# Six batches of attention results multiplied by the reciprocals of their sums in the second part of the kernel, behind the load, and the ones matmuls taking GpSimd's sum last

## The chip, the cores and the metric

The kernel runs on one core of a Trainium2 chip. The metric is the device time of that core in microseconds (us), the median of the runs shown. Times within one execution come from a hardware profile of a single run. TensorE is called PE (its weight loads PEld), VectorE DVE, ScalarE ACT, GpSimd POOL, and SyncE, which only issues DMAs here, SP.

## The reference, cut to what matters

```python
# q, k, v: (8 batches, 8 heads, 1152, 64)
q_pool = q.reshape(B, H, 576, 2, 64).mean(axis=3)
scores = scale * q_pool @ k.T
attn   = exp(scores - max(scores)) / (sum(exp(...)) + 1e-9)
x      = attn @ v                         # as (8, 576, 512)
theta  = x @ w_theta
y      = w_tok_r @ (x * cos(theta)) + w_tok_i @ (x * sin(theta))
u      = x + y
out    = u + max(u @ w_ch, 0)
```

The division by the sum can be made anywhere between the matmul with v and the first use of x. Where it is made is what this case is about.

## The kernel before

**Part one** is the attention, for 32 pairs of heads, four pairs to a batch, one after the other in steps of about 25 us. The matmuls of a pair are the row maxima (`pm`, `px`, `py`; reduced by DVE into `mx`), the scores (`pe`), the weighted values (`pa`), and a few matmuls with ones (`pns`) that sum the exponentials over partitions. ACT writes the exponentials (`pc`), POOL adds seven of the nine `pc` tiles of each half into `ss` (L443), and the ones matmuls take `ss` and the last two `pc` tiles (L479).

From the sums, a chain of small steps makes the factors: `norm_spread` and `norm_load` turn the row of sums through DRAM, DVE takes the reciprocal (`rc`, L506), `norm_save` stores it (`ro`), `norm_bcast` (L519) reads it back with two DMAs into all 128 partitions (`dn`, 128x576), `norm_out` (L528) multiplies the pair's result `xu` by it on DVE, and `norm_store` (L542) stores `xu` in DRAM as `xd[b]`.

**Part two** is the rest, batch by batch, in cycles of about 55 us. `xload` (L183, L186) loads a batch as `xT` (128 x 4 slices x 640 columns for an even batch, which also holds the last 64 columns of the next one; 576 for an odd one) into one of two tiles. `xhi` (ACT, L196) and `xlo` (POOL, L200) split each slice in two for the theta matmuls (`pth`, L844); `xblock` (DVE, L825) transposes it in blocks of 32 for a store to `xbd[b]` (L826), from where `xnload` (L834) fetches it in the other layout. A chain on DVE and ACT (L866 to L901) makes the products `Z`, POOL their low halves (L905); the token matmuls (`py`, L932) add them up, `uadd` (L948) adds `xT`, the channel matmuls (`pr`, L971) and `relu` (L984) follow, and `oblock` (L992, L995) transposes and stores the output. So `uadd` of batch b - 2 is the last to read the `xT` tile that batch b gets.

All five engines work in the order in which the program is written. That order is made by numbers: each step is entered with a position (`at` in part one, 18 positions a pair; `at2` in part two, 56 positions a batch) and the steps are written in order of their positions. SP too is one queue: a DMA that waits for its data holds back every DMA written behind it. PE's banks of PSUM are handed on in turn, so a late reader (`relu`, `uadd`, a DVE maximum) makes a later matmul wait.

## Time and profile before

| | |
|---|---|
| median of 3 runs | 1280.24 us (1278.96 to 1281.43) |
| the profiled execution, whole | 1281.45 us |
| its span in the profile | 1279.7 us |
| PE busy over the span | 1237.6 us, 97% |
| DVE, ACT, POOL busy | 942.3, 671.6, 746.2 us |
| part one (until the last `pns`) | 0 to 834 us |
| part two | 834 to 1280 us |

The profiled execution is 1.21 us above the median, and 1.75 us of it lie outside the span. The profile's chain of work that ended last is 82% PE; busy shares of the other engines are averages over two parts that load them differently. POOL is at work most of part one and little in part two, DVE 86% of part one and some 60% of part two.

### The profile page before, as it was taken

The page shows a single profiled execution, that of the slowest core. Times are in us where ns is not written, and L with a number is a line of the kernel's source. Part 1 is how long each engine was busy: PE and PEld are TensorE (multiplying, and loading weights), DVE is VectorE, ACT ScalarE, POOL GpSimd, SP SyncE. Part 2 cuts the span into 40 slices and gives each one's busy share as a digit, 9 for nine tenths or more (in the row PEclk, how much of TensorE's full clock was granted, in tenths as well). Part 3 has the DMA queues.
Part 4 walks back from the last instruction along what each step waited for, and adds up shares of the span by engine and source line. Part 5 has one row for each costly group of instructions (what it writes and reads, how often), then busy time and mean ns, then how long its engine had stood idle before and what let it go on. Part 6 is the DMA issues. An engine that isn't in the chain of part 4 may idle for free.

```text
span 1279.7 us, 29400 instructions
## 1 busy us (share of the span) xinstructions
PE 1237.6 (97%) x11619; PEld 1002.2 (78%) x11619; DVE 942.3 (74%) x1370; ACT 671.6 (52%) x1161; POOL 746.2 (58%) x536
## 2 busy tenths in 40 slices
PE   3999999999999999999999999999999999999998
PEld 2777777767777777777777677788999999999998
DVE  6878888888888888888888887455565656647453
ACT  1566566656656665665666565555443443444331
POOL 0598768787786878787787767624323233232320
PEclk7999999999999999999999999999999999999999
DMA  5746554556555465555556541324635435354332
GB/s 92 129 84 129 105 115 109 120 118 143 107 105 116 102 130 113 110 104 123 107 116 113 106 89 52 99 74 108 134 49 127 90 76 128 49 132 83 81 54 38
DMA packets 488763, 129.88 MB, mean 101 GB/s; under 512 B 458672, under 2 KB 459632, under 8 KB 488624
## 3 DMA queue, kind: packets, MB, share of 16 engines
q1 hardware_dynamic: 488624, 127.99, 48.3%
q8 instruction: 91, 1.49, 0.5%
q14 instruction: 48, 0.39, 0.1%
HBM read 97.21 MB, written 29.52 MB: 99 GB/s over the span
## 4 chain that ended last, share of the span: by engine, by line
PE 82%; DVE 10%; DMA 3%; issue 3%; ACT 1%; SPq 1%; POOL 0%; DVEq 0%; ACTq 0%; POOLq 0%
PE pa L457 19%; PE pe L430 19%; PE py L932 17%; PE pr L971 8%; PE pth L844 8%; PE pm L375 6%; DVE mx L382 4%; PE pns L479 4%; DVE qk L292 2%; DMA qk<-in_k_dram 2%; PE px L392 1%; DVE wf L601 1%; DVE mx L397 1%; DMA nmr<-nt 1%; DMA qn<-in_q_dram 1%
## 5 line engine op out<-in xcount | busy, mean ns | idle before, releaser
L443 POOL TENSOR_TENSOR ss<-ss,pc 128x576 f32<-128x576 f32 x314 | 463.6, 1477 | 52.5 <-ACT pc L433 32.2
L382 DVE TENSOR_REDUCE mx<-pm 128x2 f32<-128x768 f32 x384 | 356.7, 952 | 96.0 <-PE pm L375 94.5
L433 ACT ACTIVATE pc<-pe 128x576 f32<-128x576 f32 x576 | 349.7, 652 | 74.7 <-PE pe L430 61.3
L457 PE MATMUL pa<-pc,vn 128*64 128x288 f32 x2304 | 300.4, 410 | 0.4 <-ACT pc L433 0.4
L457 PEld LDWEIGHTS pa<-pc,vn 128*64 128x64 f32 x2304 | 156.8, 137 | 108.8 <-issue 5.7
L932 PE MATMUL py<-wtk,Z 128*128 128x288 f32 x1728 | 233.8, 296 | 0.0
L932 PEld LDWEIGHTS py<-wtk,Z 128*128 128x128 f32 x1728 | 232.3, 189 | 1.3
L905 POOL TENSOR_TENSOR Z<-ab,Z 128x512 fp32r<-128x512 f32 x40 | 52.1, 1302 | 259.4 <-ACT Z L901 221.9
L430 PE MATMUL pe<-hi 64*128 64x288 f32 x1152 | 182.0, 311 | 0.3 <-DVE lo L360 0.2
L430 PE MATMUL pe<-nmr,oner 64*128 64x288 f32 x1152 | 171.2, 292 | 0.0
L430 PE MATMUL pe<-lo,hi 64*128 64x288 f32 x1152 | 170.6, 291 | 0.0
L430 PE MATMUL pe<-hi,lo 64*128 64x288 f32 x1152 | 170.6, 291 | 0.0
L443 POOL TENSOR_TENSOR ss<-pc,pc 128x576 f32<-128x576 f32 x64 | 91.7, 1433 | 126.0 <-ACT pc L433 125.6
L375 PE MATMUL pm<-hi 64*128 64x384 f32 x768 | 145.8, 377 | 16.1 <-ACT hi L349 5.8
L430 PEld LDWEIGHTS pe<-hi 64*128 64x128 f32 x1152 | 109.2, 185 | 24.1 <-issue 7.5
L375 PEld LDWEIGHTS pm<-hi 64*128 64x128 f32 x768 | 73.2, 187 | 64.0 <-DVE mx L382 16.5
L349 ACT CAST hi<-pt 128x768 fp32r<-128x768 f32 x64 | 56.2, 879 | 114.0 <-DVE pt L321 105.4
L430 PEld LDWEIGHTS pe<-lo,hi 64*128 64x128 f32 x1152 | 109.9, 186 | 0.0
L430 PEld LDWEIGHTS pe<-hi,lo 64*128 64x128 f32 x1152 | 109.4, 185 | 0.0
L430 PEld LDWEIGHTS pe<-nmr,oner 64*128 64x128 f32 x1152 | 109.1, 185 | 0.0
L971 PEld LDWEIGHTS pr<-us,wch 128*128 128x128 f32 x768 | 104.2, 188 | 1.6
L971 PE MATMUL pr<-us,wch 128*128 128x288 f32 x768 | 105.2, 296 | 0.0
(100 smaller groups left out, 1417.6 us busy)
## 6 DMA issues: line engine op xcount, KB each, us to landing
vn<-in_v_dram SPq DMA_DIRECT2D x32, 576.0 KB
qn<-in_q_dram SPq DMA_DIRECT2D x124, 144.0 KB
qk<-in_k_dram SPq DMA_DIRECT2D x124, 144.0 KB
dn<-ro SPq DMA_DIRECT2D x64, 144.0 KB
xd<-xu SPq DMA_DIRECT2D x32, 288.0 KB
xT<-xd SPq DMA_DIRECT2D x8, 1152.0 KB
xn<-xbd SPq DMA_DIRECT2D x140, 64.0 KB
out_dram<-ub SPq DMA_DIRECT2D x124, 72.0 KB
```

What stands on the lines that cost most here:

```text
L349: nc.scalar.copy(hi, src)
L375: nc.tensor.matmul(pm[:, h, 0:W], hi[hs, Q0 + j * P : Q0 + (j + 1) * P], hi[hs, K0[3 * g] : K0[3 * g] + W], start=True, stop=True,)
L382: nc.vector.tensor_reduce(mx[:, j : j + 5 : 4, g : g + 1], pm[:, :, 0:W], AX.X, ALU.max)
L430: nc.tensor.matmul(pe[:, h, 0:HALF], w[hs], x[hs], start=(n == 0), stop=(n == 3))
L433: nc.scalar.activation(pcs[u, kt], pe[:, :, 0:HALF], AF.Exp, scale=SC)
L443: eng.tensor_tensor(st["ss", u], first, st["pc"][u, kt], ALU.add)
L457: nc.tensor.matmul(pa[hs, 0, 0:HALF], st["vn"][:, h, (kt + 3) % KT, :], st["pc"][u, kt][:, h, :], start=(kt == 0), stop=(kt == KT - 1),)
L479: nc.tensor.matmul(px[a : a + 32, 1, 0:HALF], ones, sets[u][n][:, h, :], start=(n == 0), stop=(n == len(sets[0]) - 1), tile_position=(0, a),)
L844: nc.tensor.matmul(th, xs[c][:, j * P : (j + 1) * P], ws[:, c], start=(n == 0), stop=(n == 11))
L905: engine("zlo", b).tensor_tensor(Z[1], t, Z[0].bitcast(F32), ALU.subtract)
L932: nc.tensor.matmul(st["py", c, u][:, 0:HALF], Z[zi][:, c * P : (c + 1) * P], wtk[wi][:, kw, u * HALF : (u + 1) * HALF], start=(i == 0 and ...
L971: nc.tensor.matmul(pr[u][:, 0:HALF], wch[wi][:, c, e * P : (e + 1) * P], st["us", ui][:, c, u * HALF : (u + 1) * HALF], start=(n == 0), st ...
```

## The change

Three things change. First, the order of the ones matmuls: the `pc` tiles come first, `ss` last. Second, for pairs 8 to 31 (batches 2 to 7) `norm_bcast` and `norm_out` are left out of part one: the reciprocals are stored in a DRAM tile that is kept (`rod[b]`), and `xu` is stored as it is. Third, in part two each of these batches is loaded earlier (position -79.5, was -64.6), and for each of its four slices the factors are loaded into one tile `dn` (`dnload`: four DMAs for an even batch, two for an odd one) and multiplied onto `xT` by DVE (`dnmul`) before the slice is split and transposed. The tile `dn` is a single buffer, shared with `x4`, so a `dnload` waits for the `dnmul` before it. `xblock` moves from -57 by steps of 1 to -55 by steps of 1.4.

```diff
-XB_AT = -57.0
+XB_AT = -55.0
+DN_AT = (-79.5, 6.8, 6.4)
...
-            sets = [[st["ss", u]] + [st["pc"][u, kt] for kt in range(tail, KT)] for u in range(2)]
+            sets = [[st["pc"][u, kt] for kt in range(tail, KT)] + [st["ss", u]] for u in range(2)]
...
+            if i < 2 * NP:
+                rdo = st["ro"] = dram.tile([4, HALF], F32, tag="ro", name=f"ro{i}", bufs=2)
+            else:
+                rdo = rod[b][hp]
...
-                if n != "norm_turn" or 4 <= i < 8:
+                if n == "norm_turn" and not NP <= i < 2 * NP:
+                    continue
+                if i < 2 * NP or n not in ("norm_bcast", "norm_out"):
                     at(base + pl[n], 9, fn, i)
...
+        def dnload(b, c):
+            dn = bst["dn", b, c] = xp.tile([P, 5 * P], F32, tag="dn", name=f"dn{b}_{c}")
+            for m in range(2 - b % 2):
+                rv = rod[b + m][c].rearrange("(h u) c -> h (u c)", h=2)
+                for h in range(2):
+                    src = rv[h : h + 1, 4 * P * m : SQ]
+                    nc.sync.dma_start(
+                        dn[h * D : (h + 1) * D, (SQ if m else 0) : (5 * P if m else SQ)],
+                        src.broadcast_to([D, SQ - 4 * P * m]),
+                    )
+
+        def dnmul(b, c):
+            x = bst[b]["xT"][:, c, 0 : SQ if b % 2 else 5 * P]
+            nc.vector.tensor_tensor(x, x, bst["dn", b, c][:, 0 : SQ if b % 2 else 5 * P], ALU.mult)
...
-                at2(base + PLAN2["xload"] if b > 1 else X1_AT, xload, b)
+                at2(base + DN_AT[0] if b > 1 else X1_AT, xload, b)
+                for c in range(ND if b > 1 else 0):
+                    at2(base + DN_AT[0] + 0.1 + DN_AT[1] * c, dnload, b, c)
+                    at2(base + DN_AT[0] + DN_AT[2] + DN_AT[1] * c, dnmul, b, c)
...
-                        at2(base + XB_AT + c, xblock, b, c)
+                        at2(base + XB_AT + 1.4 * c, xblock, b, c)
```

SP's queue in part two, around the load of batch 4, which is an even one (`xn_3` and `xn_4` belong to batch 3, the stores `out_dram` to batch 2, `xbd` is the first transposed slice of batch 4; a row with x4 is four DMAs). Before:

```order
L834 DMA xn_3_14222<-xbd_93 32x16x32 x4
L995 DMA out_dram<-ub_0_14229 192x3x32 x4
L834 DMA xn_4_14284<-xbd_93 32x16x32 x4
L995 DMA out_dram<-ub_1_14322 192x3x32 x4
L995 DMA out_dram<-ub_2_14332 192x3x32 x4
L183 DMA xT_12040<-xd_86 128x4x576
L186 DMA xT_12040<-xd_87 128x4x64
L995 DMA out_dram<-ub_3_14383 192x3x32 x4
L826 DMA xbd_94<-xb_0_14394 128x576
```

and now, from the load on:

```order
L185 DMA xT_11944<-xd_86 128x4x576
L188 DMA xT_11944<-xd_87 128x4x64
L828 DMA dn_0_14111<-rod_102 64x576 x2
L828 DMA dn_0_14111<-rod_103 64x64 x2
L857 DMA xn_3_14157<-xbd_93 32x16x32 x4
L1018 DMA out_dram<-ub_0_14164 192x3x32 x4
L828 DMA dn_1_14173<-rod_102 64x576 x2
L828 DMA dn_1_14173<-rod_103 64x64 x2
L857 DMA xn_4_14225<-xbd_93 32x16x32 x4
L1018 DMA out_dram<-ub_1_14263 192x3x32 x4
L1018 DMA out_dram<-ub_2_14274 192x3x32 x4
L828 DMA dn_2_14280<-rod_102 64x576 x2
```

The load now stands ahead of `xn_3`, and of the four groups of factors (two DMAs of 576 columns and two of 64 each) the first stands right behind it, the second and third behind the stores of batch 2 as they come; the fourth follows the last of those stores.

DVE in the same place, from the third transposed result of batch 2 on (`ab` and `ti` are products of batch 3, `xb` the transposes of batch 4). Before:

```order
L992 STREAM_TRANSPOSE ub_2_14332<-uT_13973 128x576
L895 TENSOR_TENSOR ab<-xn_3_14222,ab 128x512
L895 TENSOR_TENSOR ti<-xn_3_14222,ti 128x512
L984 SCALAR_TENSOR_TENSOR uT_13973<-pr_30_14353,uT_13973 128x288
L984 SCALAR_TENSOR_TENSOR uT_13973<-pr_31_14354,uT_13973 128x288
L992 STREAM_TRANSPOSE ub_3_14383<-uT_13973 128x576
L895 TENSOR_TENSOR ab<-xn_4_14284,ab 128x512
L825 STREAM_TRANSPOSE xb_0_14394<-xT_12040 128x576
L825 STREAM_TRANSPOSE xb_1_14400<-xT_12040 128x576
L825 STREAM_TRANSPOSE xb_2_14403<-xT_12040 128x576
L825 STREAM_TRANSPOSE xb_3_14423<-xT_12040 128x576
```

and now:

```order
L1015 STREAM_TRANSPOSE ub_2_14274<-uT_13901 128x576
L918 TENSOR_TENSOR ab<-xn_3_14157,ab 128x512
L918 TENSOR_TENSOR ti<-xn_3_14157,ti 128x512
L1007 SCALAR_TENSOR_TENSOR uT_13901<-pr_30_14298,uT_13901 128x288
L1007 SCALAR_TENSOR_TENSOR uT_13901<-pr_31_14299,uT_13901 128x288
L1015 STREAM_TRANSPOSE ub_3_14328<-uT_13901 128x576
L835 TENSOR_TENSOR xT_11944<-xT_11944,dn_2_14280 128x640
L918 TENSOR_TENSOR ab<-xn_4_14225,ab 128x512
L848 STREAM_TRANSPOSE xb_0_14348<-xT_11944 128x576
L848 STREAM_TRANSPOSE xb_1_14380<-xT_11944 128x576
L835 TENSOR_TENSOR xT_11944<-xT_11944,dn_3_14339 128x640
L848 STREAM_TRANSPOSE xb_2_14396<-xT_11944 128x576
```

The third and fourth multiplication of batch 4 stand between batch 2's last results, the last `ab` of batch 3 and the transposes; the first two stand earlier, behind the first and second result of batch 2 and what goes with them.

PE at the ones matmuls of pair 1, before:

```order
L479 MATMUL pns_1158<-ss_1_749,ones 32x288
L479 MATMUL pns_1158<-ss_1_948,ones 32x288
L479 MATMUL pns_1158<-ss_1_749,ones 32x288
L479 MATMUL pns_1158<-ss_1_948,ones 32x288
L479 MATMUL pns_1158<-pc_07_751,ones 32x288
L479 MATMUL pns_1158<-pc_17_950,ones 32x288
L479 MATMUL pns_1158<-pc_07_751,ones 32x288
L479 MATMUL pns_1158<-pc_17_950,ones 32x288
L479 MATMUL pns_1158<-pc_08_768,ones 32x288
L479 MATMUL pns_1158<-pc_18_966,ones 32x288
L479 MATMUL pns_1158<-pc_08_768,ones 32x288
L479 MATMUL pns_1158<-pc_18_966,ones 32x288
```

and now:

```order
L481 MATMUL pns_1166<-pc_07_759,ones 32x288
L481 MATMUL pns_1166<-pc_17_958,ones 32x288
L481 MATMUL pns_1166<-pc_07_759,ones 32x288
L481 MATMUL pns_1166<-pc_17_958,ones 32x288
L481 MATMUL pns_1166<-pc_08_776,ones 32x288
L481 MATMUL pns_1166<-pc_18_974,ones 32x288
L481 MATMUL pns_1166<-pc_08_776,ones 32x288
L481 MATMUL pns_1166<-pc_18_974,ones 32x288
L481 MATMUL pns_1166<-ss_1_757,ones 32x288
L481 MATMUL pns_1166<-ss_1_956,ones 32x288
L481 MATMUL pns_1166<-ss_1_757,ones 32x288
L481 MATMUL pns_1166<-ss_1_956,ones 32x288
```

The eight `pc` rows now stand ahead of the four `ss` rows. ACT and POOL keep their order.

## Rows read from the trace of the kernel before

**Rows 1.** Windows: busy us by engine (instructions), PE's granted clock, DMA share, GB/s

```profile
894.00:897.10 3.10, 3.07 (x9) 2.40 (x10) 2.85 (x5) 1.62 (x3) 0.37 (x1) 0.61 0.17 26
992.00:1024.00 32.00, 32.00 (x224) 30.91 (x223) 21.42 (x38) 14.52 (x24) 9.13 (x7) 1.00 0.47 91
```

**Rows 2.** Waits of PE, whole span: us in total, times, longest

```profile
PE px L392 <- DVE mx L382: 9.6, 18, 0.6
```

**Rows 3.** Groups by line and shape: busy us, mean ns, idle before and releaser

```profile
L528 DVE TENSOR_TENSOR xu<-xu,dn 128x576 f32<-128x576 f32 x32 | 28.3, 884 | 6.0 <-DMA dn<-ro 6.0
...
L479 PEld LDWEIGHTS pns<-ss,ones 128*32 128x32 f32 x256 | 5.2, 108 | 6.9 <-ACT pc L433 4.9 <-issue 1.9
...
L200 DVE TENSOR_TENSOR xl<-xT,xh 128x640 fp32r<-128x640 f32 x3 | 4.7, 1568 | 0.1
```

**Rows 4.** Timeline of DVE in part one: start, us, instruction, idle before and releaser

```profile
411.71 0.74 DVE L528 TENSOR_TENSOR xu<-xu,dn 128x576 f32<-128x576 f32 x1
...
414.22 0.96 DVE L382 TENSOR_REDUCE mx<-pm 128x2 f32<-128x768 f32 x1 [0.69 <-PE pm L375]
...
427.02 0.96 DVE L382 TENSOR_REDUCE mx<-pm 128x2 f32<-128x768 f32 x1 [1.17 <-PE pm L375]
427.90 1.45 DVE L292 TENSOR_TENSOR qk<-qn 128x576 f32<-128x576 f32 x1
```

**Rows 5.** Timeline of PE in part one, a `px` that waits

```profile
405.51 0.73 PE L392 MATMUL px<-hi,tail 128*128 128x512 f32 x3 [0.61 <-DVE mx L382]
```

**Rows 6.** Timeline of all engines at the end of part one, pair 30's factors

```profile
826.75 1.10 SPq L519 DMA_DIRECT2D dn<-ro  x2
830.57 0.76 DVE L528 TENSOR_TENSOR xu<-xu,dn 128x576 f32<-128x576 f32 x1 [5.99 <-DMA dn<-ro]
```

**Rows 7.** Timeline of DVE ahead of batch 4's transposes

```profile
997.95 1.54 DVE L948 TENSOR_TENSOR uT<-xT,py 128x288 f32<-128x288 f32 x4
...
1006.80 0.68 DVE L895 TENSOR_TENSOR ti<-xn,ti 128x512 f32<-128x512 f32 x1
1008.76 0.43 DVE L868 TENSOR_SCALAR kk<-kk 128x512 f32<-128x512 f32 x1 [1.28 <-ACT kk L866]
...
1013.15 0.82 DVE L984 SCALAR_TENSOR_TENSOR uT<-pr,uT 128x288 f32<-128x288 f32 x2 [0.53 <-PE pr L971]
...
1017.20 0.78 DVE L992 STREAM_TRANSPOSE ub<-uT 128x576 f32<-128x576 f32 x1
1018.63 0.69 DVE L895 TENSOR_TENSOR ab<-xn,ab 128x512 f32<-128x512 f32 x1 [0.65 <-POOL Z L905]
```

**Rows 8.** Timeline of SP's issues there

```profile
1005.82 2.63 SPq L995 DMA_DIRECT2D out_dram<-ub  x4
1008.56 2.18 SPq L834 DMA_DIRECT2D xn<-xbd  x4
1011.61 5.83 SPq L995 DMA_DIRECT2D out_dram<-ub  x8
```

**Rows 9.** Timeline of all engines from batch 4's load to its theta matmuls

```profile
1017.54 0.57 SPq L183 DMA_DIRECT2D xT<-xd  x1
...
1020.05 1.29 POOL L905 TENSOR_TENSOR Z<-ab,Z 128x512 fp32r<-128x512 f32 x1 [1.42 <-ACT Z L901]
1023.81 0.78 DVE L825 STREAM_TRANSPOSE xb<-xT 128x576 f32<-128x576 f32 x1 [4.49 <-DMA xT<-xd]
...
1025.00 6.15 POOL L200 TENSOR_TENSOR xl<-xT,xh 128x640 fp32r<-128x640 f32 x4 [3.66 <-ACT xh L196]
...
1030.68 2.02 PE L844 MATMUL pth<-wth,xh 128*128 128x512 f32 x8
...
1032.54 1.09 PE L844 MATMUL pth<-wth,xl 128*128 128x512 f32 x4
```

**Rows 10.** Timeline of PE in part two

```profile
894.03 3.26 PE L844 MATMUL pth<-wth,xh 128*128 128x512 f32 x8 [2.10 <-DVE r L870]
...
1016.28 13.90 PE L932 MATMUL py<-wtk,Z 128*128 128x288 f32 x103
```

More of the change, by code (lines that the diff above doesn't have):

```diff
@@ L140, in pooled_attention_moe_kernel @@
     xbd = [dram.tile([DM, SQ], F32, name=f"xbd{b}") for b in range(B)]
+    rod = [dram.tile([NP, 4, HALF], F32, name=f"rod{b}") for b in range(B)]
     def bank(kind, name):
@@ L816, in xturn @@
             pt = st["xp", j] = bank(XN0_BANK[j], f"pxn{j}")
[L817 removed]
+            xs = bst["x4"] if j == 4 else st["xT"][:, :, j * P : (j + 1) * P]
             for c in range(ND):
```

6 lines of the change are left out of this document (3 added, 3 removed).

## The prediction

> **What bounds the kernel now.** I read the windows first: in part two PE is busy 32.00 of 32.00 us at the full clock [rows 1]; the ten other windows of this length from 896 to 1248 us read 32.00 too. An edit there can gain nothing unless it shortens PE's own work, and it loses whatever it makes PE wait. Then the waits of PE: in part one the one wait that repeats is a `px` matmul held up by a DVE maximum, 9.6 us in 18 places [rows 2, 5]. In part two the one wait of note is 2.10 us at 894 us, after which PE ran the next theta matmuls at a granted clock of 0.61, a mix of its two levels, 1.2 and 2.4 GHz: eight of them took 3.26 us, against 2.02 at full clock [rows 1, 9, 10]. So such a wait costs 2.10 + 1.24 = 3.3 us. The waits of 0.6 us in part one cost only themselves.
>
> **The ones matmuls.** The same twelve matmuls, in another order. The gain could be a wait for POOL's `ss`. The row of the first ones shows idle time of the weight loads behind ACT and issue, 6.9 us over the span, and none behind POOL [rows 3]. PE's own list shows no wait there. Worth 0, and I give it no range of its own.
>
> **Part one without factors.** Out go 24 multiplications of 0.884 us, 21.2 us of DVE's time [rows 3], and 48 broadcast DMAs of 1.10 us a pair on SP [rows 6]. What is that worth to PE? Only what it takes from the waits in [rows 2]. In the steps I looked at, the multiplication stands at 411.71; soon after it DVE is idle, waiting for PE, at 414.22, and again for 1.17 us at 427.02 [rows 4]. The late maxima come out of a run of DVE that begins only then: a maximum, then the query pooling at 427.90, 1.45 us long, then more maxima, and `px` waits. The time that DVE saves is lost in its idle time before that run. I take 0; the bound is all of [rows 2], -9.6 us. PE's work is unchanged, and nothing is added here: SP's queue only gets shorter, and `norm_store` no longer waits for DVE.
>
> **Part two: the load moved and the factors added.** Each of six batches gets four multiplications and 16 (even) or 8 (odd) DMAs, 72 in all. Prices: a multiplication of 576 columns takes 0.76 when POOL rests [rows 6], so one of 640 some 0.84; two-input operations of 640 columns at the end of part one, where POOL worked too, took 1.57 [rows 3]. Two factor DMAs take SP 1.10, so four take 2.2; the factors were there 830.57 - 827.85 = 2.7 us after the last issue [rows 6]. DVE's total, 24 times 0.84 to 1.57, is 20 to 38 us, in an engine with a third of its time free [rows 1]; what matters is who is held up. I walk through batch 4 by the times of before.
>
> *First factor.* The load waits for `uadd` of batch 2, done at 997.95 + 1.54 = 999.5 [rows 7]. Two loads and four factor DMAs keep SP until 1002.8. A load needs 6.3 us (1017.54 to 1023.81 [rows 9]), so it is there at 1005.8, the factors behind it by 1007. DVE comes at 1006.80 + 0.68 = 1007.5 and its 0.84 fit into the 1.28 that it idled before 1008.76 [rows 7]. Cost 0. Behind SP's wait for `uadd` stands batch 3's fourth `xn` load, whose products DVE makes behind 1013.15.
>
> *Second.* Its DMAs follow the stores that end at 1008.45 [rows 8], take until 1010.65 and land at 1013.4; they also wait for the first multiplication, which is done. DVE arrives at 1012.6, waits 0.8, and is done at 1014.2, so `relu` slides from 1013.15 to 1014.2 and ends at 1015.0 [rows 7]. The next taker of its bank is the token matmul at 1016.28 [rows 10]. Cover 1.3 us, cost 0.
>
> *Third.* The `xn` load behind it slides to 1012.8 [rows 8]; four stores until 1015.5, four more, which wait for `relu`'s tile, from 1015.8 to 1018.4; then the factors until 1020.6. The last two are short, so they land between 1022.2 and 1023.3. DVE idles from about 1019 until then; before, it idled 4.49 in this place, waiting for the load itself [rows 9]. The multiplication ends at 1023.0 to 1024.1. Behind it stands `ab` (before, 1018.63), and POOL is free 2.7 us after its start (1020.05 + 1.29 - 1018.63 [rows 7, 9]): 1025.7 to 1026.8. The last token slice, made by this `ab`, is needed after 96 of 108 matmuls from 1016.28 to 1030.68, at 1029.1 [rows 9, 10]: cover over 2 us. POOL's four subtractions, before from 1025.00, now end 6.15 later, at 1031.9 to 1033.0. PE needs the fourth three matmuls of 0.23 after 1032.54, at 1033.2 [rows 9]. Cover 0.2 to 1.3 us.
>
> *Fourth.* The last stores end at 1023.3 on SP, then the factors wait for the third multiplication: issued by 1025.5 to 1026.3, landed at 1027.1 to 1029.0, multiplied (0.84 to 1.57) by 1027.9 to 1030.6, split by ACT in 0.7 by 1028.6 to 1031.3. PE needs it as the fourth matmul from 1030.68, at 1031.4. Cover 0.1 to 2.8 us. The transposes and `uadd` behind it come within 1 us of their old times, and PE takes `uadd`'s banks only after the theta matmuls, three us later.
>
> So in an even batch all covers hold, two of them barely. POOL's 6.15 may also grow by what a multiplication in its midst costs, up to 1.57 - 0.84 = 0.7, which would use up 0.2 and make PE wait 0.5. Between 0 and +0.5 a batch, three batches, I take +0.3 in all, nearer to none, since the landings of [rows 6] are the nearest to these. Odd batches put two DMAs where an even one puts four: SP is 1.1 us earlier at each step, and I take 0 there.
>
> **A rule that speaks against it.** What the rows show is that a two-input DVE operation beside POOL takes 0.7 longer [rows 3, 6]. The Trainium skill, page "SBUF — State Buffer", section "Who interferes with whom", says that a DVE instruction with two SBUF inputs and a GpSimd instruction that reads SBUF lock each other out: the second waits until the first is done. Here that would put the fourth multiplication's 0.84 whole into POOL's four subtractions, and `Z`'s last half behind the third. By the rows: 3 x 0.84 = 2.5 us at most where the cover is used up, a rival below. No row shown here tells which of the two gives way.
>
> **The sum.** The profiled execution took 1281.45, 1.21 above the median. 0 - 0 + 0.3 = +0.3 makes 1281.75 of it, or 1280.5 as a median.
>
> **The rivals.**
>
> *The third factors come late (slower).* One mechanism: SP's queue gives them out behind eight stores and an `xn` load, DVE stands still on them, and behind DVE stand `ab`, POOL and the theta matmuls. It decides when they land later than 1023.5 in batch 4 (and as late in batches 2 and 6): each us beyond is a us of PE. For it: the cover of 0.2 to 1.3. Against it: DVE stood still there before, until 1023.81, and PE did not wait. Price: 3 x 0.9 = 2.7 to 3 x 3.3 = 10 us, if each wait grows to 2.1 and takes the clock down: 1283 to 1290.
>
> *The lock.* As above, up to 2.5 us: 1280.5 to 1283.
>
> *DVE's relief reaches PE in part one (faster).* -9.6 us if all `px` waits go: 1271. For it: 21 us less on the engine that PE waits for. Against it: the idle time between the multiplication and the late run [rows 4].
>
> *The wait at 894 us goes (faster).* It lies in a loop of PE, ACT and DVE in batch 1, where pair 31's multiplication is gone 50 us before. If the loop shifts, -3.3: 1277. Against it: DVE waits for ACT several times in between, so that the shift dies out.
>
> **How the numbers follow.** My forecast, PE's work as it was and no wait over half a us: 0.65. Late third factors 0.17, the lock 0.06 (half within 0.2%), `px` waits gone 0.05, the wait at 894 gone 0.07. About 0.2% (2.6 us) is what a measurement of this kernel can tell from no change. Faster 0.05 + 0.07 = 0.12; slower 0.17 + 0.03 = 0.20; same 0.68. The range from 1277.0 to 1286.5 takes in the forecast, the lock, the wait at 894 gone and the lower half of the late factors; it leaves out the rest of these (some 0.08) and the `px` case (0.05), and some of what I have not thought of.
>
> **What would show it.** Right: 24 multiplications gone from part one, with pair after pair starting at the old distances and the `px` waits near 9.6; DVE idle 3 to 5 us before each even batch's third multiplication; PE 32.00 of 32.00 after 900 us. Wrong: theta matmuls that wait for POOL's `xl` or ACT's `xh` in batches 2, 4, 6, a granted clock under 1.00 after 900 us, or `px` waits under 5 us.

## The result

The kernel after took 1290.89 us in the median of 4 runs (1288.14 to 1293.46), the kernel before 1279.99. The ratio is 1.0077, with a 95% interval of 1.0064 to 1.0090: slower by about 9.9 us by the ratio (the two medians lie 10.9 us apart). The forecast of 1280.5 us was too low, and so was the upper end of its range, 1286.5. The profiled execution of after took 1293.46 us, with a span of 1291.7; its trace ends 12.03 us later than that of before, so it shows a little more of the loss than the median does.

Part one answers to the forecast: part two starts at 834.66 us in after and at 835.01 in before, 0.35 earlier. I then compared the start of every group of theta matmuls in the two traces. But for 0.6 us in batch 1, where a theta matmul waits for POOL's `xl`, the offset grows only in batches 2, 4 and 6:

| stretch | after minus before, us |
|---|---|
| up to the wait at 894 us | +0.2 (batch 1 included) |
| batch 2, from there to its second theta group | +1.9 (a gain of 2.2 and a loss of 4.1) |
| batch 4 | +5.0 |
| batch 6 | +4.8 |
| batches 3, 5 and 7 | 0.0 each |

The waits of PE in after (us in total, times, longest), where `px` answers to [rows 2]:

```profile
PE px L394 <- DVE mx L384: 9.6, 18, 0.6
...
PE pth L867 <- ACT xh L198: 7.7, 3, 3.0
...
PE pth L867 <- DVE r L893: 2.1, 1, 2.1
```

The `px` waits are what they were, to the tenth of a microsecond. New are three waits of the theta matmuls for ACT's `xh`, one in each of the three batches.

PE, ACT and DVE in batch 4 of after (start, us, instruction, what ended the idle time before it). The first two rows answer to [rows 9, 10]:

```profile
1018.42 15.33 PE L955 MATMUL py<-wtk,Z 128*128 128x288 f32 x108
1033.59 0.86 PE L867 MATMUL pth<-wth,xh 128*128 128x512 f32 x3
1036.88 2.14 PE L867 MATMUL pth<-wth,xh 128*128 128x512 f32 x5 [2.43 <-ACT xh L198]
1038.83 1.91 PE L867 MATMUL pth<-wth,xl 128*128 128x512 f32 x4
```

```profile
1030.90 1.98 ACT L198 CAST xh<-xT 128x640 fp32r<-128x640 f32 x3
1036.11 0.72 ACT L198 CAST xh<-xT 128x640 fp32r<-128x640 f32 x1 [3.23 <-DVE xT L835]
```

```profile
1010.23 1.80 DVE L835 TENSOR_TENSOR xT<-xT,dn 128x640 f32<-128x640 f32 x1 [0.31 <-DMA xn<-xbd]
...
1017.75 0.83 DVE L835 TENSOR_TENSOR xT<-xT,dn 128x640 f32<-128x640 f32 x1 [0.99 <-DMA dn<-rod]
1018.49 0.82 DVE L1007 SCALAR_TENSOR_TENSOR uT<-pr,uT 128x288 f32<-128x288 f32 x2
...
1028.91 0.82 DVE L835 TENSOR_TENSOR xT<-xT,dn 128x640 f32<-128x640 f32 x1 [5.72 <-DMA dn<-rod]
...
1034.20 1.88 DVE L835 TENSOR_TENSOR xT<-xT,dn 128x640 f32<-128x640 f32 x1 [2.39 <-DMA dn<-rod]
```

Read it from the bottom up. DVE stands 5.72 us in front of the third multiplication and 2.39 in front of the fourth, each time until the factors land. ACT has three slices split at 1032.9 and waits for the fourth. PE makes three theta matmuls of the twelve, waits 2.43 us for the fourth `xh`, and then runs slowly. Windows of PE in after (us, PE busy and its matmuls, granted clock, DMA share, GB/s):

```profile
894.00:897.10 3.10, 2.85 (x12) 1.00 1.17 122
...
1033.59:1036.90 3.31, 0.88 (x6) 1.00 0.40 156
1036.90:1041.00 4.10, 4.10 (x12) 0.58 0.45 157
```

After the wait the granted clock is 0.58, near the lower of the two levels (1.2 of 2.4 GHz). Between the first and the second theta group of batch 4, PE loses 4.28 us against before: 2.43 of waiting and some 1.8 by the clock. Another 0.76 goes ahead of the theta matmuls, in a `py` that takes 15.33 us for 108 matmuls. Some 0.6 of it is a wait of the weight loads (PEld) for `relu` (L1007), which stands on DVE behind the second multiplication, itself late by its factors:

```profile
PEld py L955 <- DVE uT L1007: 0.6, 2, 0.4
```

Batches 2 and 6 repeat the wait for the fourth `xh` (2.27 and 3.01 us) and the slow matmuls behind it, but not this `py`. By the trace the three batches lose some 14 us: 7.7 of waiting for `xh`, about 5.5 by the clock behind these waits, and 0.8 here. The wait at 894 us, which in after is not followed by slow matmuls, gives 2.2 us back.

Why the factors are late stands on SP's queue (after, batch 4; compare [rows 8]):

```profile
1001.71 0.38 SPq L185 DMA_DIRECT2D xT<-xd  x1
1002.13 0.51 SPq L188 DMA_DIRECT2D xT<-xd  x1
1002.68 2.53 SPq L828 DMA_DIRECT2D dn<-rod  x4
1005.26 5.03 SPq L857 DMA_DIRECT2D xn<-xbd  x4
1010.40 2.66 SPq L1018 DMA_DIRECT2D out_dram<-ub  x4
1013.16 2.50 SPq L828 DMA_DIRECT2D dn<-rod  x4
1015.70 2.17 SPq L857 DMA_DIRECT2D xn<-xbd  x4
1017.97 5.38 SPq L1018 DMA_DIRECT2D out_dram<-ub  x8
1023.40 2.55 SPq L828 DMA_DIRECT2D dn<-rod  x4
1026.05 3.28 SPq L1018 DMA_DIRECT2D out_dram<-ub  x4
1029.76 2.41 SPq L828 DMA_DIRECT2D dn<-rod  x4
```

SP issues almost without a pause from 1001.7 to 1032.2. The four `xn` behind the load take 5.03 us; ten microseconds later four of them take 2.17, as they did in [rows 8]. One by one, with the row of SP's waits from 1000 to 1012 us:

```profile
1005.26 1.11 SPq L857 DMA_DIRECT2D xn<-xbd  x2
...
1008.01 0.30 SPq L857 DMA_DIRECT2D xn<-xbd  x1
...
1009.17 1.12 SPq L857 DMA_DIRECT2D xn<-xbd  x1
```

```profile
SPq L857 <- DMA xT<-xd: 2.5, 2, 1.6
```

The third `xn` is issued 0.02 us after the load has landed (1007.99, from the times at which its semaphore was counted up), the fourth 0.02 us after the load's second DMA (1009.15). No data passes from the load of batch 4 to the `xn` of batch 3. The tie is in the program: its DMAs from SP and ScalarE get eight completion semaphores in turn, and a DMA waits for the one that had its semaphore before, eight DMAs ahead (in the trace the semaphores 101 to 104 and 107 to 110 come round on these two queues).

So 2.5 of the 5.03 us are waits for the load's semaphores. The tie is not all of it. The kernel before issues four stores right behind the load of its batch; none of the four waits for a DMA, and they take 4.86 us, where four stores elsewhere take 2.63 [rows 8]:

```profile
1018.77 4.86 SPq L995 DMA_DIRECT2D out_dram<-ub  x4
```

DMAs that SP issues while a load is under way thus took longer without any wait on a semaphore. What the tie costs by itself is not shown.

### The profile page after: what moved, and what is told of

It reads as the page before. It is cut to its first block, busy times and chain, and to the rows that moved or that the text cites. A ratio compares the mean times of both kernels' runs of the same rounds, so it can differ in the third digit from the quotient of the medians.

```text
span 1291.7 us, 29374 instructions
## 1 busy us (share of the span) xinstructions
PE 1241.3 (96%) x11619; PEld 1003.4 (78%) x11619; DVE 947.5 (73%) x1370; ACT 672.5 (52%) x1161; POOL 747.9 (58%) x536
## 4 chain that ended last, share of the span: by engine, by line
PE 73%; DVE 12%; DMA 4%; issue 4%; SPq 4%; ACT 3%; POOL 1%; DVEq 0%; ACTq 0%; POOLq 0%
PE pa L459 19%; PE pe L432 18%; PE py L955 12%; PE pth L867 6%; PE pr L994 6%; PE pm L377 6%; DVE mx L384 4%; PE pns L481 4%; DMA dn<-rod 2%; DVE qk L294 2%; DMA qk<-in_k_dram 1%; SPq L828 1%; PE px L394 1%; SPq L1018 1%; DVE mx L399 1%
## 5 line engine op out<-in xcount | busy, mean ns | idle before, releaser
L384 DVE TENSOR_REDUCE mx<-pm 128x2 f32<-128x768 f32 x384 | 356.9, 953 | 110.7 <-PE pm L377 109.5
```

The source lines that it names most:

```text
L384: nc.vector.tensor_reduce(mx[:, j : j + 5 : 4, g : g + 1], pm[:, :, 0:W], AX.X, ALU.max)
```

## The experiments

All ratios are to the kernel before, run on the same chip in the same session, with 95% intervals. The diffs are cut to what matters (`...` marks a gap), and those of e7_poolq, e12_actq and e16_poolfac to e18_mul1 show only the differing part of some lines. Line numbers of kernels with added lines are higher by four (L839 for L835, L852 for L848).

### The parts of the change alone

**e1_ones** has the new order of the ones matmuls and nothing else.

```diff
-            sets = [[st["ss", u]] + [st["pc"][u, kt] for kt in range(tail, KT)] for u in range(2)]
+            sets = [[st["pc"][u, kt] for kt in range(tail, KT)] + [st["ss", u]] for u in range(2)]
```

> The kernel before with only the other order of the ones matmuls (GpSimd's sum last); nothing else of the change. Theory (the factors in the second part carry the whole loss, the ones order is worth nothing because the wait at the px matmuls ends with VectorE's mx): 1278 to 1282 us, ratio 0.999 to 1.001, PE's waits px<-DVE mx stay at 9 to 10 us. Rival (the ones order gives something in part one that part two takes away again): 1270 to 1277 us with px waits under 5 us.

Measured: 1280.99 us, ratio 0.9996 (0.9986 to 1.0005). The order is worth nothing that can be measured.

**e2_nofactor** leaves out the factors' transfers and multiplications.

```diff
-                for c in range(ND if b > 1 else 0):
+                for c in range(0):
```

> The kernel after without the factors' loads and multiplications in the second part: the results of the last six batches stay undivided, so that part of the computation is left out; the earlier load of the block, the moved xb and the lighter first part stay. Theory (the stalls of batches 2, 4 and 6 come from the factors, which arrive late through SP's queue and hold VectorE): stalls at the starts of batches 2, 4, 6 go, 1275 to 1281 us. Rival (the earlier load alone does it, by holding up SP's queue and so the xn and out transfers, or by its traffic): 1286 to 1294 us, stalls of 4 us or more stay at the three batches.

Measured: 1281.14 us, ratio 0.9998 (0.9989 to 1.0008). All of the loss goes with the factors. The early load alone costs nothing, although SP's issues behind it are longer here too:

```profile
1000.89 4.29 SPq L857 DMA_DIRECT2D xn<-xbd  x4
```

SP waits for no DMA among these four, so the tie is not the cause here. The same run shows that the lighter part one is worth nothing, since it has 21 us less of DVE's work there and gains none of it.

**e13_mulonly** keeps the multiplications and loads one factor tile once; **e14_loadonly** keeps the transfers and leaves out the multiplications.

```diff
 e13_mulonly
-                    at2(base + DN_AT[0] + 0.1 + DN_AT[1] * c, dnload, b, c)
+                    if b == 2 and c == 0:
+                        at2(base + DN_AT[0] + 0.1 + DN_AT[1] * c, dnload, b, c)
...
-            nc.vector.tensor_tensor(x, x, bst["dn", b, c][:, 0 : SQ if b % 2 else 5 * P], ALU.mult)
+            nc.vector.tensor_tensor(x, x, bst["dn", 2, 0][:, 0 : SQ if b % 2 else 5 * P], ALU.mult)
 e14_loadonly
-                    at2(base + DN_AT[0] + DN_AT[2] + DN_AT[1] * c, dnmul, b, c)
```

> The kernel after with all its multiplications in their places, but only one factor tile loaded, once (the results are multiplied with wrong factors; the other transfers of factors are left out). Theory (transfers on SP's queue carry the loss, VectorE's 24 multiplications of some 0.8 us lie in its idle time): 1279 to 1283 us, no theta stall. Rival (VectorE's time carries a part): 1284 to 1289 us.

> The kernel after with all transfers of factors in their places, but without the multiplications (the results of the last six batches stay undivided). No engine reads the factors, so that what is left is SP's issue time alone. Theory A (the lateness of the factors is all, since VectorE waits for them): 1279 to 1282 us. Theory B (the issue time pushes out and xb transfers back, as in e9_mul3, and that costs by itself): 1283 to 1289 us, VectorE waiting for out_dram<-ub 2 us or more in batches 2, 4 and 6.

Measured: the multiplications alone 1281.69 us, ratio 1.0004 (0.9995 to 1.0013); the transfers alone 1284.69 us, ratio 1.0030 (1.0018 to 1.0041). The third and fourth multiplication of batch 4 in e13_mulonly:

```profile
1018.67 1.90 DVE L835 TENSOR_TENSOR xT<-xT,dn 128x640 f32<-128x640 f32 x1
...
1023.90 1.51 DVE L835 TENSOR_TENSOR xT<-xT,dn 128x640 f32<-128x640 f32 x1
```

Both are about twice as long as the 0.82 us of the first two, since GpSimd works beside them, and still PE waits for nothing after 900 us but for 0.2 us at the end, as in before. The Trainium skill, page "SBUF — State Buffer", section "Who interferes with whom", lets such a pair lock each other out; the lengthening agrees with that, and it cost nothing that can be measured here.

In e14_loadonly nobody reads the factors, and yet 3.8 us (0.0030 of 1280) are lost. DVE's waits there from 850 to 1200 us (us in total, times, longest), and PE's matmuls behind batch 4's theta:

```profile
DVE xb L848 <- DMA out_dram<-ub: 23.8, 9, 5.5
DVE xb L848 <- DMA xbd<-xb: 17.9, 6, 4.2
DVE ub L1015 <- DMA out_dram<-ub: 4.9, 2, 2.5
```

```profile
1034.53 8.95 PE L955 MATMUL py<-wtk,Z 128*128 128x288 f32 x60 [0.49 <-DVE uT L971]
```

The transposes `xb` take their tiles from the same pair of buffers as the results' transposes `ub`, and those tiles are free only when the stores have read them. The stores stand behind the factors on SP's queue. So `xb` is late, `uadd` behind it on DVE is late (1034.06 in e14_loadonly), and the 60 token matmuls that need its banks take 8.95 us, where the kernel before took 8.15. That is expectation B, in its lower half. For comparison, e2_nofactor, without the transfers, has 13.9 us of DVE's waits for stores in front of `xb` in the same stretch and none in front of `ub`.

By their times the multiplications alone cost 0.5 us (interval -0.6 to 1.7) and the transfers that no one waits for 3.8; some 5.6 of the 9.9 us come only when both are there, that is, when DVE waits for factors. These are not parts of one sum: e14_loadonly loses its 3.8 us at `uadd` and behind it, and in after PE waits nowhere for `uadd`, since its theta matmuls wait first.

### Why the factors are late

**e3_xnfirst** puts the load and the first two factors behind the four `xn`.

```diff
-                at2(base + DN_AT[0] if b > 1 else X1_AT, xload, b)
+                at2(base - 75.3 if b > 1 else X1_AT, xload, b)
...
-                    at2(base + DN_AT[0] + 0.1 + DN_AT[1] * c, dnload, b, c)
+                    at2(base + max(DN_AT[0] + 0.1 + DN_AT[1] * c, -75.2), dnload, b, c)
```

> The kernel after with the block's load and the first two factors put behind the four xn transfers of the batch ahead on SP's queue, in place of ahead of them (some 4 us later in the program); the third and fourth factors stay where they were. Theory (SP's queue is held up behind the load: the four xn took 5.03 us in place of 2.18, and the factors behind them are late by that): the third factor of batch 4 lands 2 to 3 us earlier, the stalls of batches 2, 4, 6 shrink by 1 to 3 us each, 1281 to 1287 us. Rival (the third and fourth factors are late for another reason, the two buffers that they share with the first two or VectorE's own load): within 0.2% of after, 1288 to 1293 us.

Measured: 1304.58 us, ratio 1.0178 (1.0163 to 1.0193). Both expectations missed: it became worse. I had left the multiplications in their places, so that DVE came to the first one before its factors were issued. SP and DVE in batch 4:

```profile
1003.57 1.90 SPq L857 DMA_DIRECT2D xn<-xbd  x4
...
1014.05 7.78 SPq L828 DMA_DIRECT2D dn<-rod  x8
```

```profile
1018.61 0.82 DVE L835 TENSOR_TENSOR xT<-xT,dn 128x640 f32<-128x640 f32 x1 [5.33 <-DMA dn<-rod]
```

One thing it does show: ahead of the load, the four `xn` take 1.90 us. The 5.03 in after come with the load, by the tie or by its traffic.

**e6_place** keeps the one buffer and moves the third and fourth factors forward on SP's queue, and the multiplications ahead of them on DVE.

```diff
-                    at2(base + DN_AT[0] + 0.1 + DN_AT[1] * c, dnload, b, c)
-                    at2(base + DN_AT[0] + DN_AT[2] + DN_AT[1] * c, dnmul, b, c)
+                    at2(base + (DN_AT[0] + 0.1 + DN_AT[1] * c if b % 2 or c < 2 else (-68.15, -60.35)[c - 2]), dnload, b, c)
+                    at2(base + (DN_AT[0] + DN_AT[2] + DN_AT[1] * c if b % 2 or c in (0, 3) else (-68.2, -60.4)[c - 1]), dnmul, b, c)
```

> The kernel after with its one buffer for the factors, and only the place of the second and third multiplications and of the third and fourth factors' transfers changed for batches 2, 4 and 6: the third factor ahead of the eight out transfers on SP's queue, the fourth ahead of the next four. Theory (place behind the out transfers is the larger part of the lateness): third factor of batch 4 lands some 4 to 5 us earlier, the fourth 2 to 3, stalls shrink by 2 to 4 us each, 1281 to 1286 us. Rival (each transfer waits anyway for the multiplication that frees the buffer, and VectorE now stands at the second one): 1288 to 1300 us.

Measured: 1293.63 us, ratio 1.0094 (1.0079 to 1.0109). The third factors come in time, and the theta waits are gone, but nothing is won. DVE stands at the second multiplication, in front of `relu`, and PE waits there, before `py`:

```profile
1017.21 0.83 DVE L835 TENSOR_TENSOR xT<-xT,dn 128x640 f32<-128x640 f32 x1 [3.54 <-DMA dn<-rod]
...
1023.78 0.82 DVE L835 TENSOR_TENSOR xT<-xT,dn 128x640 f32<-128x640 f32 x1
```

```profile
1018.46 5.21 PE L994 MATMUL pr<-us,wch 128*128 128x288 f32 x24 [2.33 <-DVE uT L1007]
...
1020.80:1023.60 2.80, 2.80 (x15) 0.59 0.54 86
```

The last line is a window: the granted clock is 0.59 behind this wait too. The rival's mechanism was right, and so was its time.

Four buffers of their own for the factors (e4_four, expected at 1276 to 1282 us) have no room in SBUF: the last pool wants 16 KB per partition and 9.1 are left, so there is no time for them.

**e10_bufonly** gives the factors buffers (the second to fourth land in the `xl` tiles, which are free at that time) and leaves their places; **e5_xlbuf** moves them forward as well.

```diff
-            dn = bst["dn", b, c] = xp.tile([P, 5 * P], F32, tag="dn", name=f"dn{b}_{c}")
+            if b % 2 or c == 0:
+                dn = xp.tile([P, 5 * P], F32, tag="dn", name=f"dn{b}_{c}")
+            else:
+                dn = xhl[1][c].bitcast(F32)
+            bst["dn", b, c] = dn
...
 e10_bufonly
-                    at2(base + DN_AT[0] + 0.1 + DN_AT[1] * c, dnload, b, c)
+                    at2(base + (-71.2 if c == 1 and b % 2 == 0 else DN_AT[0] + 0.1 + DN_AT[1] * c), dnload, b, c)
 e5_xlbuf
-                    at2(base + DN_AT[0] + 0.1 + DN_AT[1] * c, dnload, b, c)
+                    at2(base + (DN_AT[0] + 0.1 + DN_AT[1] * c if b % 2 or c == 0 else (-71.2, -69.1, -67.0)[c - 1]), dnload, b, c)
```

> The kernel after with the second to fourth factors of batches 2, 4 and 6 in the xl tiles, each transfer left at the place on SP's queue that it has in the kernel after (only the second moves by 1.4 us in the plan, with no other transfer between). Tells the one buffer apart from the place on the queue. If the buffer is the cause: 1281 to 1287 us, as e5_xlbuf or better. If the place behind the out transfers is: 1287 to 1292 us, the third factor still lands some 2.8 us behind an issue at 1023 to 1025 in batch 4.

> The kernel after, where the second to fourth factors of batches 2, 4 and 6 land in the block's own xl tiles, which stand free from the last theta of the batch ahead until GpSimd writes them, so that no transfer waits for the one buffer of the factors, and are issued earlier on SP's queue (the second ahead of the last xn, the third ahead of both out transfers, the fourth between them). The multiplications keep their number and their place. Theory (PE loses 4 us or more at each of these batches because VectorE stands waiting for the third and fourth factors, which come late through the one buffer and SP's queue): VectorE's waits for factors fall from 5.7 and 2.4 us in batch 4 to under 0.5 us, the three stalls go, 1277 to 1283 us. Rival (the four multiplications and their transfers would cost that even in time, by VectorE's own time, the lock of the shared port, or the out and xn transfers pushed back): 1286 to 1293 us.

Measured: buffers alone 1289.05 us, ratio 1.0059 (1.0040 to 1.0078); buffers and places 1287.38 us, ratio 1.0042 (1.0025 to 1.0059). The buffers alone can't be told apart from after: the third factors still come behind the eight stores, and DVE stands 5.57 us for them in batch 4. With the places too, some 4.5 us come back, less than theory said; the time is the rival's. DVE in e5_xlbuf, batch 4:

```profile
1024.88 0.78 DVE L839 TENSOR_TENSOR xT<-xT,xl 128x640 f32<-128x640 f32 x1
...
1029.92 0.78 DVE L852 STREAM_TRANSPOSE xb<-xT 128x576 f32<-128x576 f32 x1 [3.66 <-DMA out_dram<-ub]
1032.78 0.78 DVE L852 STREAM_TRANSPOSE xb<-xT 128x576 f32<-128x576 f32 x1 [2.08 <-DMA out_dram<-ub]
1033.48 0.78 DVE L839 TENSOR_TENSOR xT<-xT,xl 128x640 f32<-128x640 f32 x1
```

The third and fourth multiplication wait for no factor any more. DVE waits for the stores instead, which the earlier factors push back (one of the rival's reasons), and the fourth multiplication stands behind two such waits.

**e9_mul3** is e5_xlbuf with the fourth multiplication of these batches ahead of the four `xb`; **e12_actq** is e9_mul3 with the second to fourth factors issued from ScalarE's queue.

```diff
 e9_mul3
-                    at2(base + DN_AT[0] + DN_AT[2] + DN_AT[1] * c, dnmul, b, c)
+                    at2(base + (-56.0 if c == 3 and b % 2 == 0 else DN_AT[0] + DN_AT[2] + DN_AT[1] * c), dnmul, b, c)
 e12_actq
-                    nc.sync.dma_start(
+                    (nc.sync if b % 2 or c == 0 else nc.scalar).dma_start(
...
-(-71.2, -69.1, -67.0)[c - 1]
+(-68.95, -68.9, -65.0)[c - 1]
```

> e5_xlbuf with one thing more: in batches 2, 4 and 6 the fourth multiplication stands ahead of the four transposes xb on VectorE, where it stood between the second and the third. In e5_xlbuf the factors were there in time, but VectorE stood 3.66 and 2.08 us in batch 4 in front of the xb transposes, whose tiles the later out transfers still held, and the fourth multiplication behind them came to 1033.48. Theory (that wait is what is left of the loss): the fourth xh comes at or before 1030 in batch 4, the theta stalls go, 1280 to 1283 us. Rival (the factors cost it by VectorE's own time even so): 1285 to 1288 us as in e5_xlbuf.

> e9_mul3 with the transfers of the second to fourth factors of batches 2, 4 and 6 issued from ScalarE's queue, in stretches in which ScalarE was idle in e9_mul3 (4.3 us from 1010 in batch 4, 2.6 us from 1016), so that SP's queue carries 7.3 us less in each of these batches. Theory (what is left of the loss is SP's issue time, which pushes the out transfers back, and these hold the ub tiles in front of VectorE's transposes): VectorE's waits for out_dram<-ub fall under 1 us, 1279 to 1283 us. Rival (VectorE's own multiplications are what is left): 1285 to 1290 us. Third case (ScalarE's issues hold up its own ab and xh): above 1288 us, with PE waiting for ScalarE.

Measured: e9_mul3 1288.97 us, ratio 1.0060 (1.0045 to 1.0076); e12_actq 1287.30 us, ratio 1.0047 (1.0030 to 1.0065). In e9_mul3 the fourth `xh` comes in time and no theta matmul waits for it, as theory said, but it is not faster than e5_xlbuf and missed both of its ranges: `xb` and `uadd` are now behind the fourth multiplication, and PE waits for `uadd` (`py` for `uT`, 3.4 us in 2 places). e12_actq's time is in the range of its rival. SP has fewer DMAs to issue, and yet the four `xn` behind the load took 7.97 us. SP's waits from 1000 to 1012 us in e12_actq:

```profile
SPq L861 <- DMA xl<-rod: 3.3, 1, 3.3
SPq L861 <- DMA dn<-rod: 1.6, 1, 1.6
SPq L861 <- DMA xT<-xd: 1.5, 1, 1.5
```

So SP's `xn` waited for factors that ScalarE had issued: the two queues share the eight semaphores. Moving DMAs to ScalarE saves SP's issue time and keeps the tie. The theory of SP's issue time as the whole of the rest falls with this run; the reason of its rival, DVE's own time, falls with e13_mulonly.

### The tie cut

GpSimd's DMAs have semaphores of their own. **e15_poolload** is after with the load of batches 2 to 7 issued by GpSimd. **e16_poolfac** is e9_mul3 with the second to fourth factors of batches 2, 4 and 6 issued by GpSimd, in a stretch in which it was idle; **e17_poolboth** does both; **e18_mul1** is e17_poolboth with the second multiplication behind the third `relu`.

```diff
 e15_poolload, e17_poolboth, e18_mul1
-        nc.sync.dma_start(xT[:, :, 0:SQ], xv)
+        (nc.gpsimd if b > 1 else nc.sync).dma_start(xT[:, :, 0:SQ], xv)
...
 e16_poolfac, e17_poolboth, e18_mul1
-                    nc.sync.dma_start(
+                    (nc.sync if b % 2 or c == 0 else nc.gpsimd).dma_start(
...
-(-71.2, -69.1, -67.0)[c - 1]
+(-70.7, -70.69, -70.68)[c - 1]
 e18_mul1
-at2(base + (-56.0 if c == 3 and b % 2 == 0 else
+at2(base + ({1: -65.5, 3: -56.0}[c] if c % 2 and b % 2 == 0 else
```

> The kernel after with only the load of batches 2 to 7 issued from GpSimd's queue, which has completion semaphores of its own; the factors stay on SP with their one buffer. Theory (the xn behind the load took 5.03 us because each DMA waits until the one eight before it, here the load, has landed): the four xn take 2.2 to 2.6 us, SP's later issues in batch 4 come 2.5 to 3 us earlier, DVE's wait for the third factor falls from 5.7 to about 3 us, 1283 to 1287 us. Rival (the load's own traffic holds up the DMAs behind it, or GpSimd's queue starts it later): within 2 us of after, 1289 to 1293 us, or above.

> e9_mul3 with the second to fourth factors of batches 2, 4 and 6 issued from GpSimd's queue, in a stretch of 7.3 us in which GpSimd was idle, with semaphores of its own; e12_actq did the same from ScalarE's queue, but on the eight semaphores that SP uses. Theory (the eight semaphores in turn are what tied stores and xn to the factors): SP's stores in batch 4 stand less, DVE's waits for stores fall to those of e2_nofactor (13.9 us in front of xb, none in front of ub, from 850 to 1200 us), 1279 to 1283 us. Rival (the factors' transfers themselves delay stores and xn on the shared DMA engines, or GpSimd's Z comes late behind its issues): 1285 to 1290 us as e12_actq, or PE waiting for POOL's Z.

> e16_poolfac with the load issued from GpSimd's queue as well. Theory: no slower than e16_poolfac, 1278 to 1283 us, no wait of PE beyond those of before. Rival (transfers themselves, or GpSimd's issues, which hold its Z): 1284 to 1291 us.

> e17_poolboth with the second multiplication of batches 2, 4 and 6 behind the third relu and its transpose on DVE, where it stood ahead of them and waited 2.6 to 3.7 us for its factors, which GpSimd's queue lands late. Theory (the loss is a chain of waits of DVE for transfers in front of something PE needs, and this is the last of them): PE's waits for uT in front of py go, 1279 to 1283 us, equal to before. Rival (the transfers cost 3 to 4 us by themselves wherever they are issued): 1284 to 1287 us.

Measured:

| kernel | us | ratio to before |
|---|---|---|
| e15_poolload | 1291.09 | 1.0081 (1.0055 to 1.0108) |
| e16_poolfac | 1285.04 | 1.0037 (1.0024 to 1.0050) |
| e17_poolboth | 1285.00 | 1.0028 (1.0016 to 1.0040) |
| e18_mul1 | 1281.41 | 1.0010 (1.0001 to 1.0020) |

e15_poolload missed its theory, and its time is in the range of its rival. SP waits there for no semaphore of the load, so that tie is cut. It is no test of what the tie costs, though: the four `xn`, which took 1.90 us, were issued by 1003.5, and the load from GpSimd's queue started only at 1004.15. DVE still stood 5.22 us for the third factor. The first four stores had to wait for DVE's results and took 3.33 us in place of 2.66, and of the queue's delay only some 1.6 us were won at the third factors. The runs spread from 1288.37 to 1295.32, and the median can't be told apart from that of after. The profiled run is the fastest of them: PE's waits for `xh` are 4.4 us in place of 7.7, and the granted clock stays at 1.00 behind them. The slower runs have no trace.

e16_poolfac and e17_poolboth missed the upper ends of their theories by 2 us. The times are at the rivals' lower ends, but not by the rivals' mechanism: PE waits for no `Z`. In e16_poolfac DVE waits 9.3 us for stores in front of `xb`, and no longer in front of `ub`. What was left stood at the second multiplication, whose factors land late from GpSimd's queue, and PE paid for it at `relu` (e16_poolfac, batch 4):

```profile
1017.89 0.83 DVE L839 TENSOR_TENSOR xT<-xT,xl 128x640 f32<-128x640 f32 x1 [2.65 <-DMA xl<-rod]
...
1019.14 14.62 PE L959 MATMUL py<-wtk,Z 128*128 128x288 f32 x106 [1.80 <-DVE uT L1011]
```

e18_mul1 moves that multiplication behind the `relu` in question. PE's waits of `py` for `relu`, 3.2 us in 3 places in e17_poolboth, are gone, and so is the loss but for 1.3 us (0.0010 of 1280, interval 0.1 to 2.6; it just overlaps that of e17_poolboth). DVE still stands for factors there, 1.82 us in batch 4, but at a place where PE needs nothing of it. The trace of e18_mul1 has its 1.4 us ahead of 894 us; from there to the end no theta group loses anything against before. It still moves the same data and makes the same multiplications. So the transfers have no price of their own here beyond this, at most 2.6 us by the interval; what cost 9.9 us is DVE standing in front of them, at places where PE comes next.

### The wait in part one

**e7_poolq** is the kernel before with the query pooling moved ahead of the first maximum of a pair; **e8_both** is e5_xlbuf with that, **e11_all** e9_mul3, **e19_best** e18_mul1.

```diff
-'pool_q': -40.262
+'pool_q': -41.35
```

> The kernel before with only VectorE's pooling of q (L292) put one place earlier in each pair of the first part, ahead of the first mx of the pair, into idle time of VectorE. Theory (PE's 18 waits for px, 9.6 us, end with a run of VectorE that starts after idle time and is 1.45 us too long because of L292, so that VectorE's freed time further ahead is worth nothing): the px waits shrink to under 3 us, 1271 to 1277 us. Rival (the wait is set by PE's own pm tiles or ScalarE's hi, which this does not move): 1279 to 1282 us.

> The kernel after with both: the factors of batches 2, 4 and 6 in the xl tiles, and the pooling of q ahead of the first mx. Theory (both hold, and the lighter first part of the kernel after now has nothing behind it): 1268 to 1277 us, below before. Rival (they share the loss, or neither holds): 1279 to 1293 us.

> e9_mul3 with the pooling of q ahead of the first mx as in e7_poolq. Theory (the change is worth nothing in either part even when its factors come in time, and e7_poolq's gain is its own): 1275 to 1279 us, the same as e7_poolq. Rival (the first part, without the factors' multiplications there, gains more once the px wait is gone): 1268 to 1274 us.

> e18_mul1 with the pooling of q ahead of the first mx, as in e7_poolq. Theory (the change, at no cost, also brings nothing): 1275 to 1279 us, the same as e7_poolq (1276.8). Rival (DVE's 21 us saved in part one are worth something once the pooling is out of the way): 1270 to 1274 us, faster than e7_poolq.

Measured: e7_poolq 1276.76 us, ratio 0.9962 (0.9947 to 0.9977); e8_both 1283.45 us, 1.0020 (1.0010 to 1.0031); e11_all 1284.81 us, 1.0033 (1.0024 to 1.0042); e19_best 1277.35 us, 0.9982 (0.9972 to 0.9992). PE's waits in e7_poolq:

```profile
PE pm L375 <- DVE mx L382: 5.4, 16, 0.8
...
PE pm L375 <- DVE mx L397: 3.7, 9, 0.4
...
PE px L392 <- DVE mx L382: 0.3, 1, 0.3
```

The `px` waits fall from 9.6 us [rows 2] to 0.3, so the late run of DVE was their cause. Half of it returns as waits of `pm`: 5.4 us in place of 3.7 behind the ordinary maxima, and 3.7 in place of 0.4 behind the maximum of `px`. Part two starts 3.9 us earlier. The versions with the changed kernel gain about the same over their own base, 3.9, 4.2 and 4.1 us by the medians. So taking 24 multiplications out of part one adds nothing that can be measured even when the `px` wait is gone: e19_best, where the change costs next to nothing, is not faster than e7_poolq, which does without the change and has the lowest time of these kernels, 4.4 us below the median of before in its session. e8_both fell into its rival's range and e11_all missed both of its ranges, because their bases, e5_xlbuf and e9_mul3, had not come down to before.

## Why the prediction was wrong, step by step

*Ones matmuls, worth 0.* Right (e1_ones).

*Part one without factors, worth 0.* Right, and for the reason given: the `px` waits are 9.6 us in 18 places as before, the idle time before the maxima grew (96.0 to 110.7 us of it over the span), and it is the place of the query pooling that decides (e7_poolq).

*First factor, cost 0.* Right for PE, but not as reasoned. The load was issued where it was expected: 1001.71 less the 2.15 us that PE was behind by then is 999.6, against 999.5. The multiplication took 1.80 us beside POOL, in place of 0.84, which does not fit into the 1.28 that DVE idled; DVE's next step began 1.0 us late by the times of before, and PE waited for nothing of it.

*Second factor, cover 1.3 us, cost 0.* Wrong in batch 4, by 0.6 us. The multiplication began at 1017.75, which is 1015.6 by the times of before, where I had it done at 1014.2. So `relu` ended at 1019.3 (1017.2) and not at 1015.0, the cover was used up, and `py` waited. It is the place at which e16_poolfac and e17_poolboth lose, and which e18_mul1 mends.

*Third factor, cover 0.2 to 1.3 us.* This is the step that failed, and the mis-sized term is the arrival of the third factors by SP's queue. I had them issued by 1020.6 and landed between 1022.2 and 1023.3; they were issued by 1025.95 and landed at 1028.8, which is 1023.8 and 1026.6 by the times of before. The prediction has the last issue 10.1 us ahead of the theta matmuls; it was 6.9, 7.6 and 7.6 us in batches 2, 4 and 6, so 2.5 to 3.2 us late in each.

In batch 4 most of this is SP's time behind the load. I priced the four `xn` there at the 2.18 us of [rows 8], which were issued when no load was under way; they took 5.03. The stores behind them ended 2.5 us late, and each group of four factors took 2.5 us and not 2.2. The landing added its part: 2.84 us after the last issue, where I had 1.6 to 2.7 (no row shows the 1.6). Of the 5.03 us, 2.5 are waits for the load's semaphores, which SP's waits in the profile name; that issues behind a load are long without them too, the 4.86 us in before could have told. How the delay divides between the two stays open.

In batches 2 and 6 the four `xn` took only 2.79 and 3.10 us, and yet DVE stood 5.62 and 4.66 us for the third factors. There more comes from waits that I had not priced: in batch 2 SP waits until 897.18 for DVE's results ahead of its first stores, and in batch 6 the second factors wait until the first multiplication, 1.63 us long, frees the one buffer. This part is read from the traces and no run takes it away by itself. DVE's third multiplication in batch 4 ended 3.5 us after the upper end of my estimate, and no cover was that large.

*Fourth factor, cover 0.1 to 2.8 us.* It failed with the third, because its transfer waits for the third multiplication to free the one buffer and follows four more stores. PE's wait was for ACT's fourth `xh`, as the text had it: 2.27, 2.43 and 3.01 us, each with about 1.8 more by the clock behind it. It hid the lateness of POOL's subtractions, for which I had reckoned the cover of the third factor: they ended at 1039.0 (1036.9 by the times of before, 3.9 past my upper end).

*"The transposes and `uadd` behind it come within 1 us of their old times."* Wrong: `uadd` of batch 4 starts at 1037.35 in after, 4.8 us late by the times of before. PE waits nowhere for it in after, because the theta matmuls come first and are late themselves. It is what costs when no one waits for the factors or when they come in time (e14_loadonly, where it starts at 1034.06 against 1030.45 in before, e9_mul3, e11_all): the factors' transfers push the stores back, and the stores hold the tiles that the transposes need. I had not priced this at all. e14_loadonly has 3.8 us for it, and e18_mul1 shows that it is a matter of places and queues.

*Odd batches, 0.* Right: no offset grows in batches 3, 5 and 7. They have half of the factor DMAs.

*The rivals.* What happened is the rival "the third factors come late", by its own mechanism and beyond its own mark (1023.5). Its price of 1283 to 1290 us was 1 us short of the median. I had 3.3 us for a wait with its clock, counting the loss of eight matmuls; the waits here brought 4.1 to 4.8 each, and the drop at 894 us, which after does without, is worth 2.2 and not 1.24. Its chance, 0.17, was too small: the covers of 0.2 and 0.1 us at the lower ends were no cover against an error of 3 us in a queue of some thirty DMAs, each priced from a quieter stretch. The lock cost nothing that can be measured (e13_mulonly: 0.5 us, at most 1.7). My price for a multiplication beside POOL was a mean that mixed two of 1.93 and 1.95 beside it with one of 0.82 when it rested; in after those beside it took 1.63 to 2.07. Which of the two gives way, the trace shows for one pair: the later. The multiplication of 1010.23 began 0.18 us behind a subtraction of POOL and took 1.80; POOL's next, begun under it, took 1.87 in place of 1.29. The `px` waits did not go by themselves. The wait at 894 us stayed at 2.10 us, but the slow matmuls behind it went.

## What to carry to other kernels

Before transfers are added to a queue, read what its DMAs wait for, completion semaphores taken in turn included, since a small transfer a few places behind a large load may wait for all of it, and price issues beside a load from a row in which a load was under way; then follow the delay to the end, to the stores, the tiles that they free, and whoever takes these next. A cover of a few tenths at the end of a dozen such prices is no cover, and what an in-order engine waits for belongs behind what PE needs next, not ahead of it (e17_poolboth to e18_mul1: one instruction, ratio 1.0028 to 1.0010). Time saved on an engine counts only where it ends a wait: one instruction of each pair moved into idle time (e7_poolq) gave more than taking 21 us off that engine.

## What the runs showed of the hardware

SP's and ScalarE's DMAs were tied to each other in the program: an `xn` of SP's queue waited 3.3 us for a factor that ScalarE had issued (e12_actq). With the second queue the ratio was 1.0047 against 1.0060 without (e9_mul3), and 1.0037 with GpSimd's queue, which has semaphores of its own (111 to 118, e16_poolfac); the intervals of the three overlap. Four `xn` took 1.90 us ahead of the load (e3_xnfirst, and e15_poolload, where the load starts behind them) and 2.17 long after it. Right behind it they took 5.03 and 7.97 us in after and e12_actq, with 2.5 and 6.4 us of waits on semaphores, and 4.29 us in e2_nofactor without such a wait; four stores right behind the load in before took 4.86.

The same wait of 2.1 us at 894 us was followed by a granted clock of 0.61 in before [rows 1] and of 1.00 in after, with 2.2 us between the two; the profiled runs of e5_xlbuf, e7_poolq, e12_actq and e17_poolboth did without the drop too. So a wait of this length does not always cost the clock. The waits of 2.43 us (after), 2.33 us (e6_place), 1.94 us (e9_mul3) and 1.81 us (e11_all) did. Those of 1.3 and 1.5 us in e5_xlbuf and e9_mul3, of 1.80 us in e16_poolfac and of 2.28 us in e15_poolload did not: the granted clock stayed at 1.00 behind them. What decides between 2.1 and 2.1, or between 1.80 and 1.81, is not settled here.
